# Issue order at the change of row tiles: both weight splits first, late rows centred on ScalarE and transposed one step earlier

## The chip, the cores and the metric

The kernel runs on one core of one Trainium2 chip. The metric is the device time of one execution in microseconds (us); shorter is better. The core's engines are called as the profile calls them: PE is TensorE (matmuls, with PEld for its weight loads), DVE is VectorE, ACT is ScalarE, POOL is GpSimd, and SP issues most of the DMAs. Each engine works through its own instructions in the order in which the program gives them; an instruction that waits holds up everything behind it on that engine.

## The reference

Two stages are computed. The first is an attention with 32 packed queries, done twice; the second is a block with a two-dimensional Fourier transform, a normalisation and a feed-forward pair of matrices. Cut to what matters:

```python
p_packed = softmax(p @ k.T / 8) @ v                # 8 batches, 8 heads, 576 rows, 64 wide
x = softmax(q @ p_packed.T / 8) @ p_packed         # then (8, 576, 512)
u = x + real(fft(fft(x, axis=1), axis=2))
un = (u - mean(u)) / sqrt(var(u) + 1e-6)           # along the 512 columns
out = u + maximum(un @ w_ch1, 0) @ w_ch2           # 512 -> 2048 -> 512
```

All inputs and outputs are float32.

## The kernel before

The 8 x 576 output rows are handled as 36 blocks of 128 rows, and four blocks make a **tile**: there are 9 tiles, 0 to 8, of 512 rows. `front(b)` computes the blocks of batch `b` up to `u`. `ffn` runs one tile through the feed-forward pair, and between its steps it advances `front` of the next batch, so that the rows of the next tile come into being while the present one is multiplied.

Every float32 product that must be exact is made of three matmuls on parts: a value is split into a high part (rounded) and a low part (the rest), and high x high, high x low and low x high are added up. `split` (lines 100 to 102) makes them: ACT copies the high part, and DVE or POOL subtracts it.

- **Weights.** The two matrices are held as 16 pieces each, `w1f` and `w2f` (128 x 512). Each tile splits them anew, because the split parts would not fit: the generator `wsplits` (line 633) yields one piece at a time, ACT makes `wr_h` and POOL makes `wr_l`. The order is w1(0), w1(1), w2(0), w1(2), w2(1) and so on to w2(15), then w1(0) of the next tile. The parts share six buffers (`wr`), three pairs, so a new pair takes the place of the pair three pieces earlier.
- **Steps of a tile.** For each of the 16 values of `j`, `up(j)` does 12 matmuls of 512 columns into the bank `ph`; ACT makes `hh` of it, DVE makes `hl`; and `down(j - 1)` does 12 matmuls into four banks `acc`. PE sees up(0), up(1), down(0), up(2), down(1), ..., up(15), down(14), down(15), and then up(0) of the next tile. After `up(j)` and after `down(j - 1)` the program asks `wsplits` for one piece each. After down(15) DVE adds `acc` to `u` (line 723), four instructions, and the rows are written out.
- **Rows of the next tile.** `Turned` brings the next tile's four blocks into the layout that `up` needs: centred (`un` = u minus its mean), transposed, and split into `uh` and `ul` (`parts(i)`, ACT and DVE). A pair of blocks that was ready earlier is centred by `less_quarters` on ACT, turned on DVE and by 16 small DMAs into `raw`. A pair whose second block is computed in the present tile's last steps is called **late**: `less(i)` centres it on DVE, and `moves(i)` transposes it on PE, four 128 x 128 transposes into `untp`. Late pairs exist for the tiles 1, 2 and 3; the tiles 4 to 8 get all four blocks from `raw`.
- **Statistics.** Some steps after a block is made, ACT sums its squares (`junk`, line 208), DVE scales them, and POOL raises the result to the power -1/2 (line 212, called the power below). The result is first used when the block's own tile ends, a tile later.

Tile 0's instructions are put in order by a scheduler. From tile 1 on, PE, DVE, ACT and POOL follow the order in which the code is written (`manual_schedule`), so that the place of a call in `ffn` decides what an engine does first. In this text w2(15) is the last weight piece of a tile, w1(0)' and w1(1)' are the first two of the next, and up(0)' is its first step.

Before the change the last step of a tile (`j == 15`) stands so: up(15), split of w2(15), then for late pairs `less(2)` and `less(3)`, `parts(0)` and `parts(1)`, a step of `front` (with the powers that are due), down(14) with the transposes of block 2 behind its 9th to 12th matmul, `parts(2)`, split of w1(0)', a step, down(15) with the transposes of block 3, `parts(3)`, split of w1(1)'.

Of the kernel before, what the change touches and what calls it, by code (L numbers as in the profile page):

```python
# [13 lines left out]
AF = mybir.ActivationFunctionType  # L14
ALU = mybir.AluOpType
# [35 lines left out]
NJ = 16  # L51
# [28 lines left out]
def tile_kernel(ctx, tc, kpT, qT, v, w1, w2, tabs, tabR, tabB, tabT, sel, ident_d, out):  # L80
    nc = tc.nc
# [95 lines left out]
    u_of, stat_of, place_of, free = {}, {}, {}, list(range(NU))  # L177
# [403 lines left out]
    class Turned:  # L581
# [8 lines left out]
            k = [key for key in self.keys[2 * h:2 * h + 2] if key[0] == b and key[1] != "R"]  # L590
            return "late" if any(key[2] == 1 for key in k) else "new" if k else "old"

        def less(self, i):
            key = self.keys[i]
            self.un[i] = work.tile([P, DM], F32, tag="ln", name="un")
            nc.vector.tensor_scalar(self.un[i], u_of[key], stat_of[key][:, 1:2], None, ALU.add)

        def moves(self, i):
            un, tp = self.un[i], bank("untp")
# [34 lines left out]
    def wsplits():  # L634

        for _ in tiles:
            for n, j in [(0, 0)] + [x for j in range(1, NJ) for x in ((0, j), (1, j - 1))] + [(1, NJ - 1)]:
                hi = work.tile([P, DM], F32R, tag="wr", name="wr_h", bufs=6)
                lo = work.tile([P, DM], F32R, tag="wr", name="wr_l", bufs=6)
                split(hi, lo, (w1f, w2f)[n][:, j, :], nc.gpsimd)  # L640
                ready.append((hi, lo))
                yield

    def ffn(first, turned, step, nxt, alone, following):
        keys = turned.keys
        n = len(keys)
        T = n * P
        uh, ul = turned.hl
        acc = [psf.tile([P, DM], F32, tag=f"acc{i}", name=f"acc{i}") for i in range(n)]
        now["acc"] = acc  # L650

        def up(j):
            wh, wl = ready.pop(0)

            pool, tag = (ps, "ps") if alone and j % 2 else (psf, "ph")
            ph = pool.tile([P, 512], F32, tag=tag, name="ph")

            step = T // 2 if first == 0 and j < SPL else T
            order = sorted(range(12), key=lambda k: k % 3 == 1) if j == 0 else range(12)
            for t in (slice(i, i + step) for i in range(0, T, step)):  # L660
                for n, k in enumerate(order):
                    c, (l, r) = k // 3, ((wh, uh), (wh, ul), (wl, uh))[k % 3]
                    nc.tensor.matmul(ph[:, t], l[:, c * P:(c + 1) * P], r[:, c, t], start=(n == 0), stop=(n == 11))  # L663
            hh = work.tile([P, 512], F32R, tag="hh", name="hh")
            hl = work.tile([P, 512], F32R, tag="hl", name="hl")
            nc.scalar.activation(hh[:, :T], ph[:, :T], AF.Relu)  # L666
            nc.vector.scalar_tensor_tensor(hl[:, :T], ph[:, :T], 0.0, hh[:, :T].bitcast(F32), ALU.max, ALU.subtract)  # L667
            return hh, hl

        def down(j, hh, hl, moves=()):  # L670

            moves = list(moves)
            vh, vl = ready.pop(0)
            for i in range(n):
                w = slice(i * P, (i + 1) * P)
                for k, (l, r) in enumerate(((hh, vh), (hh, vl), (hl, vh))):
                    nc.tensor.matmul(acc[i], l[:, w], r, start=(j == 0 and k == 0), stop=(j == NJ - 1 and k == 2))  # L677
                    if moves:
                        moves.pop(0)()

        kinds = [nxt.kind(h, following) for h in range(2)] if nxt else []
        assert kinds in ([], ["new", "late"], ["old", "new"], ["old", "old"]), kinds

        prev = None
        late = "late" in kinds
        for j in range(NJ):
            last = nxt is not None and j == NJ - 1
            cur = up(j)
            next(splits, None)
            if last:  # L690
                if late:
                    nxt.less(2)
                    nxt.less(3)
                nxt.parts(0)
                nxt.parts(1)
            step(2 * j)
            if j == 11:
                for h in range(2):
                    if kinds[h:h + 1] == ["old"]:
                        nxt.less_quarters(h)  # L700
                        nxt.turn(h)
            if prev is not None:
                down(j - 1, *prev, [lambda: None] * 8 + nxt.moves(2) if last and late else ())
                if j == 13:
                    for h in range(2):
                        if kinds[h:h + 1] == ["new"]:
                            nxt.less_quarters(h)
                if last:
                    nxt.parts(2)
                next(splits, None)  # L710
            step(2 * j + 1)
            if j == 13:
                for h in range(2):
                    if kinds[h:h + 1] == ["new"]:
                        nxt.turn(h)
            prev = cur
        down(NJ - 1, *prev, nxt.moves(3) if late else ())
        if nxt:
            nxt.parts(3)
        next(splits, None)  # L720
        for i, key in enumerate(keys):
            u = u_of[key]
            nc.vector.scalar_tensor_tensor(u, acc[i], stat_of[key][:, 2:3], u, ALU.mult, ALU.add)
            nc.sync.dma_start(out[(first + i) * P:(first + i + 1) * P, :], u)
            free.append(place_of[key])
# [24 lines left out]
    ready, splits = [], wsplits()  # L750
    next(splits)
    next(splits)
    for t, (first, tk) in enumerate(tiles):

        gen = front(t + 1) if t + 1 < B else iter(())
        ended = []

        def step(i):

            next_step()  # L760
            if t > 0 and i in (0, 2):
                next(rest, None)
            elif not ended and next(gen, None) == "rest":
                ended.append(gen)
            if t == 0 and i % 2 == 0 and i // 2 + LEAD < NJ:
                load_weights(i // 2 + LEAD)
            assert i < 2 * NJ - 1 or t + 1 >= B or ended

        nxt = Turned(tiles[t + 1][1]) if t + 1 < len(tiles) else None

        with tc.manual_schedule(engines=MANUAL) if t > 0 else nullcontext():
            ffn(first, cur, step, nxt, t + 1 >= B, t + 1)
        cur, rest = nxt, gen
# [112 lines left out]
```

## Time and profile before

| | |
|---|---|
| time, median of 3 runs | 1018.25 us (1017.5 to 1019.1) |
| the profiled execution's own time | 1017.34 us |
| its span, first to last instruction | 1015.6 us |
| granted PE clock, mean over the span | 0.983 |
| DVE busy | 582.9 us (57%) |
| ACT busy | 459.2 us (45%) |
| POOL busy | 474.6 us (47%) |

A page of the profile describes one execution. In a timeline each row is one instruction, or several alike: its start in us from the start of the span, its duration, engine, line, operation, what it writes and reads, and in brackets how long the engine had been idle before it and what it had waited for. The duration of a matmul covers its way through the array, and the next one starts before it has ended; the distance from start to start says how fast PE goes. In the list of waits a row gives who waited for whom, the total, how often, and the longest. In the windows a row gives the length of a stretch, each engine's busy time in it with the number of instructions, and then the granted PE clock, the DMA engines' busy share, and GB/s.

### The profile page before, as it was taken

The page shows a single profiled execution, that of the slowest core. Times are in us where ns is not written, and L with a number is a line of the kernel's source. Part 1 is how long each engine was busy: PE and PEld are TensorE (multiplying, and loading weights), DVE is VectorE, ACT ScalarE, POOL GpSimd, SP SyncE. Part 2 cuts the span into 40 slices and gives each one's busy share as a digit, 9 for nine tenths or more (in the row PEclk, how much of TensorE's full clock was granted, in tenths as well). Part 3 has the DMA queues.
Part 4 walks back from the last instruction along what each step waited for, and adds up shares of the span by engine and source line. Part 5 has one row for each costly group of instructions (what it writes and reads, how often), then busy time and mean ns, then how long its engine had stood idle before and what let it go on. Part 6 is the DMA issues. An engine that isn't in the chain of part 4 may idle for free.

```text
span 1015.6 us, 15016 instructions
## 1 busy us (share of the span) xinstructions
PE 957.9 (94%) x5588; PEld 782.3 (77%) x5588; DVE 582.9 (57%) x1227; ACT 459.2 (45%) x936; POOL 474.6 (47%) x426
## 2 busy tenths in 40 slices
PE   4199889999999999999999999999999999999998
PEld 2177668878877888788877887788778878888886
DVE  4885864559455856578456946595558562123112
ACT  4578634444453435445444445444534453333322
POOL 3715734364345534454355434643455344445443
PEclk9599989999999999999999999999999999999999
DMA  9367401220042001300140013101410010001001
GB/s 360 114 186 277 129 1 46 94 72 1 1 130 81 1 1 58 128 1 12 56 165 1 1 57 129 47 1 46 136 50 1 22 63 1 1 27 57 0 1 42
DMA packets 28169, 65.93 MB, mean 65 GB/s; under 512 B 5494, under 2 KB 12992, under 8 KB 28096
## 3 DMA queue, kind: packets, MB, share of 16 engines
q1 hardware_dynamic: 27120, 63.53, 18.8%
q0 software_dynamic: 976, 1.44, 0.5%
q8 instruction: 44, 0.72, 0.3%
q14 instruction: 29, 0.24, 0.1%
HBM read 48.70 MB, written 9.44 MB: 57 GB/s over the span
## 4 chain that ended last, share of the span: by engine, by line
PE 71%; DVE 8%; issue 7%; POOL 5%; ACT 3%; SPq 3%; DMA 2%; DVEq 0%; POOLq 0%; ACTq 0%
PE ph L663 32%; PE acc L677 28%; POOL wr_l L102 3%; SPq L623 3%; DVE turned L410 1%; PE po L317 1%; PE s L260 1%; DVE turned L406 1%; ACT hh L666 1%; PE py L228 1%; PE py L230 1%; PE py L229 1%; PE e1tp L294 1%; DMA ubuf<-w 1%; PE pz L228 1%
## 5 line engine op out<-in xcount | busy, mean ns | idle before, releaser
L102 POOL TENSOR_TENSOR wr_l<-w1f,wr_h 128x512 fp32r<-128x512 f32 x144 | 191.0, 1329 | 355.3 <-ACT wr_h L101 350.9
L667 DVE SCALAR_TENSOR_TENSOR hl<-ph,hh 128x512 fp32r<-128x512 f32 x144 | 98.9, 687 | 324.2 <-ACT hh L666 323.9
L102 POOL TENSOR_TENSOR wr_l<-w2f,wr_h 128x512 fp32r<-128x512 f32 x144 | 191.9, 1333 | 104.0 <-ACT wr_h L101 93.9
L663 PE MATMUL ph<-uh,wr_h 128*128 128x512 f32 (+1 forms) x580 | 229.5, 396 | 11.3 <-DVE hl L667 8.9
L663 PE MATMUL ph<-uh,wr_l 128*128 128x512 f32 (+1 forms) x580 | 226.6, 391 | 4.6 <-POOL wr_l L102 4.6
L677 PE MATMUL acc<-wr_h,hh 128*128 128x512 f32 x576 | 226.4, 393 | 0.4 <-ACT hh L666 0.4
L677 PE MATMUL acc<-wr_l,hh 128*128 128x512 f32 x576 | 225.7, 392 | 0.2 <-POOL wr_l L102 0.2
L677 PE MATMUL acc<-wr_h,hl 128*128 128x512 f32 x576 | 225.2, 391 | 0.0
L663 PE MATMUL ph<-ul,wr_h 128*128 128x512 f32 (+1 forms) x580 | 221.2, 390 | 0.0
L666 ACT ACTIVATE hh<-ph 128x512 fp32r<-128x512 f32 x144 | 86.0, 597 | 289.0 <-PE ph L663 288.7
L663 PEld LDWEIGHTS ph<-uh,wr_h 128*128 128x128 f32 x580 | 109.5, 189 | 46.2 <-DVE hl L667 10.3
L663 PEld LDWEIGHTS ph<-uh,wr_l 128*128 128x128 f32 x580 | 109.3, 188 | 29.7 <-POOL wr_l L102 6.6
L677 PEld LDWEIGHTS acc<-wr_h,hh 128*128 128x128 f32 x576 | 108.3, 188 | 23.5 <-ACT wst L171 0.8
L663 PEld LDWEIGHTS ph<-ul,wr_h 128*128 128x128 f32 x580 | 109.1, 189 | 22.0 <-DVE mx L279 0.8
L677 PEld LDWEIGHTS acc<-wr_h,hl 128*128 128x128 f32 x576 | 108.1, 188 | 22.7
L677 PEld LDWEIGHTS acc<-wr_l,hh 128*128 128x128 f32 x576 | 108.2, 188 | 22.1 <-POOL wr_l L102 0.6
L101 ACT CAST wr_h<-w1f 128x512 fp32r<-128x512 f32 x144 | 88.3, 613 | 10.7 <-PE acc L677 7.2
L101 ACT CAST wr_h<-w2f 128x512 fp32r<-128x512 f32 x144 | 89.1, 619 | 8.3 <-PE ph L663 6.7
L228 PE MATMUL py<-gh,fh 128*128 128x258 f32 x64 | 18.7, 294 | 27.5 <-ACT fh L470 27.5
L208 ACT ACTIVATE junk<-ubuf,stat 128x512 f32<-128x512 f32 x36 | 25.8, 719 | 36.2 <-DVE stat L204 36.2
L212 POOL TENSOR_TENSOR stat<-stat,mhalf 128x1 f32<-128x1 f32 x36 | 25.1, 707 | 30.8 <-DVE stat L211 30.6
L102 POOL TENSOR_TENSOR gl<-turned,gh 128x516 fp32r<-128x516 f32 x16 | 25.8, 1614 | 22.4 <-ACT gh L101 21.8
(201 smaller groups left out, 1286.6 us busy)
## 6 DMA issues: line engine op xcount, KB each, us to landing
kp<-kpT SPq DMA_DIRECT2D x16, 608.0 KB, 3.9
out<-ubuf SPq DMA_DIRECT2D x36, 256.0 KB, 2.1
vt<-v SPq DMA_DIRECT2D x14, 640.0 KB, 4.5
wst<-w SPq DMA_DIRECT2D x17, 512.0 KB, 4.7
qt<-qT SPq DMA_DIRECT2D x14, 576.0 KB, 4.4
raw<-flip SPq DMA_DIRECT2D x208, 32.0 KB, 1.8
ubuf<-w SPq DMA_DIRECT2D x9, 512.0 KB, 3.6
w1f<-w SPq DMA_DIRECT2D x3, 512.0 KB, 13.6
```

The lines of the kernel that those rows point to most:

```text
L101: nc.scalar.copy(hi, src)
L102: (lo_eng or nc.vector).tensor_tensor(lo, src, hi.bitcast(F32), ALU.subtract)
L208: nc.scalar.activation(junk, u, AF.Square, bias=st[:, 1:2], scale=1.0, accum_out=st[:, 2:3])
L212: nc.gpsimd.tensor_tensor(st[:, 2:3], st[:, 2:3], mhalf, ALU.pow)
L228: nc.tensor.matmul(o, lh, rh, start=first, stop=False)
L229: nc.tensor.matmul(o, lh, rl, start=False, stop=False)
L230: nc.tensor.matmul(o, ll, rh, start=False, stop=last)
L623: nc.sync.dma_start(raw[32 * q:32 * (q + 1), a].rearrange("p n x -> p (n x)"), flip[32 * a:32 * (a + 1), q].rearrange("p n x -> p (n x)"))
L663: nc.tensor.matmul(ph[:, t], l[:, c * P:(c + 1) * P], r[:, c, t], start=(n == 0), stop=(n == 11))
L666: nc.scalar.activation(hh[:, :T], ph[:, :T], AF.Relu)
L667: nc.vector.scalar_tensor_tensor(hl[:, :T], ph[:, :T], 0.0, hh[:, :T].bitcast(F32), ALU.max, ALU.subtract)
L677: nc.tensor.matmul(acc[i], l[:, w], r, start=(j == 0 and k == 0), stop=(j == NJ - 1 and k == 2))
```

## The change

In the last step of a tile, the split of w1(0)' is issued directly behind the split of w2(15), ahead of `parts(0)` and `parts(1)` and of the step that issues the powers. `parts(3)` moves up behind `parts(2)`, ahead of down(15). Late blocks are centred by ACT instead of DVE, at the end of the last step but one. The transposes of both late blocks stand within down(14), behind its matmuls 1 to 4 and 9 to 12; down(15) has none.

```diff
-        def less(self, i):
+        def less(self, i, scalar=False):
             key = self.keys[i]
             self.un[i] = work.tile([P, DM], F32, tag="ln", name="un")
-            nc.vector.tensor_scalar(self.un[i], u_of[key], stat_of[key][:, 1:2], None, ALU.add)
+            if scalar:
+                nc.scalar.activation(self.un[i], u_of[key], AF.Identity, bias=stat_of[key][:, 1:2], scale=1.0)
+            else:
+                nc.vector.tensor_scalar(self.un[i], u_of[key], stat_of[key][:, 1:2], None, ALU.add)
...
             if last:
-                if late:
-                    nxt.less(2)
-                    nxt.less(3)
+                next(splits, None)
                 nxt.parts(0)
                 nxt.parts(1)
             step(2 * j)
...
             if prev is not None:
-                down(j - 1, *prev, [lambda: None] * 8 + nxt.moves(2) if last and late else ())
+                down(j - 1, *prev, nxt.moves(2) + [lambda: None] * 4 + nxt.moves(3) if last and late else ())
...
                 if last:
                     nxt.parts(2)
-                next(splits, None)
+                    nxt.parts(3)
+                else:
+                    next(splits, None)
+                if late and j == NJ - 2:
+                    nxt.less(2, True)
+                    nxt.less(3, True)
             step(2 * j + 1)
...
-        down(NJ - 1, *prev, nxt.moves(3) if late else ())
-        if nxt:
-            nxt.parts(3)
+        down(NJ - 1, *prev)
         next(splits, None)
```

The lines behind the edit have numbers 3 or 4 higher in the changed kernel (up's matmul is L663 before and L666 after, down's L677 and L680, `hh` L666 and L669).

On ACT, where tile 3 ends (all blocks from `raw`), the order before is this, from `hh` of up(15) to `hh` of up(0)':

```order
L666 ACTIVATE hh<-ph 128x512
L101 CAST wr_h<-w2f 128x512
L101 CAST uh<-raw 128x4x4x32 x3
L101 CAST wr_h<-w1f 128x512
L101 CAST uh<-raw 128x4x4x32
L101 CAST wr_h<-w1f 128x512
L666 ACTIVATE hh<-ph 128x512
```

In the changed kernel the same place reads:

```order
L669 ACTIVATE hh<-ph 128x512
L101 CAST wr_h<-w2f 128x512
L101 CAST wr_h<-w1f 128x512
L101 CAST uh<-raw 128x4x4x32 x4
L101 CAST wr_h<-w1f 128x512
L669 ACTIVATE hh<-ph 128x512
```

The first cast of `w1f`, that of w1(0)', has moved from behind three `uh` casts to ahead of all four.

On POOL, where tile 1 ends, the order before is this; the second w2 row is w2(15), and the two w1 rows behind the powers are w1(0)' and w1(1)':

```order
L212 TENSOR_TENSOR stat<-stat,mhalf 128x1 x2
L102 TENSOR_TENSOR wr_l<-w2f,wr_h 128x512 x2
L212 TENSOR_TENSOR stat<-stat,mhalf 128x1 x2
L102 TENSOR_TENSOR wr_l<-w1f,wr_h 128x512 x2
L102 TENSOR_TENSOR wr_l<-w2f,wr_h 128x512
```

In the changed kernel:

```order
L212 TENSOR_TENSOR stat<-stat,mhalf 128x1 x2
L102 TENSOR_TENSOR wr_l<-w2f,wr_h 128x512 x2
L102 TENSOR_TENSOR wr_l<-w1f,wr_h 128x512
L212 TENSOR_TENSOR stat<-stat,mhalf 128x1 x2
L102 TENSOR_TENSOR wr_l<-w1f,wr_h 128x512
L102 TENSOR_TENSOR wr_l<-w2f,wr_h 128x512
```

The split of w1(0)' now stands ahead of the two powers, directly behind that of w2(15); that of w1(1)' stays behind them. The order is the same where the tiles 2 to 6 end.

On ACT, where tile 1 ends (blocks 0 and 1 from `raw`, blocks 2 and 3 late), before, from the last splits of step 14 on:

```order
L101 CAST wr_h<-w2f 128x512
L208 ACTIVATE junk,stat<-ubuf,stat 128x512 x2
L666 ACTIVATE hh<-ph 128x512
L101 CAST wr_h<-w2f 128x512
L101 CAST uh<-raw 128x4x4x32 x2
L101 CAST uh<-untp 128x4x4x32
L101 CAST wr_h<-w1f 128x512
L101 CAST uh<-untp 128x4x4x32
L101 CAST wr_h<-w1f 128x512
```

And in the changed kernel:

```order
L101 CAST wr_h<-w2f 128x512
L597 ACTIVATE un<-ubuf,stat 128x512 x2
L208 ACTIVATE junk,stat<-ubuf,stat 128x512 x2
L669 ACTIVATE hh<-ph 128x512
L101 CAST wr_h<-w2f 128x512
L101 CAST wr_h<-w1f 128x512
L101 CAST uh<-raw 128x4x4x32 x2
L101 CAST uh<-untp 128x4x4x32 x2
L101 CAST wr_h<-w1f 128x512
```

Two centrings have come in ahead of the sums of squares and of `hh`, and the cast of w1(0)' has moved ahead of the `uh` casts. The order of SP's DMAs is the same in both kernels.

## The prediction

> **What bounds the kernel now.** I read the page's first part, then who waits for whom on PE, then the timeline of PE around each change of tiles, and last the other engines there.
>
> ```profile
> PE 957.9 (94%) x5588; PEld 782.3 (77%) x5588; DVE 582.9 (57%) x1227; ACT 459.2 (45%) x936; POOL 474.6 (47%) x426
> ...
> PE py L228 <- ACT fh L470: 27.5, 2, 26.0
> PE ph L663 <- DVE hl L667: 8.9, 4, 5.1
> PE ph L663 <- POOL wr_l L102: 4.6, 5, 1.5
> PE untp L603 <- DVE un L596: 1.6, 2, 0.8
> ```
>
> PE is busy 94% of the span, so only its waits and its work can be shortened. The two largest waits end, by the timeline, before tile 1 begins: they belong to the start and to tile 0, and the change leaves them alone. The last two rows are the places that it edits: five waits of up's matmul for a POOL split, and two of a transpose for DVE's centring. Here are the five, each as the first two matmuls of up(0)' (the third of the first case too):
>
> ```profile
> 509.20 0.39 PE L663 MATMUL ph<-uh,wr_h 128*128 128x512 f32 x1
> 511.12 0.50 PE L663 MATMUL ph<-uh,wr_l 128*128 128x512 f32 x1 [1.53 <-POOL wr_l L102]
> 511.46 0.39 PE L663 MATMUL ph<-uh,wr_h 128*128 128x512 f32 x1
> ...
> 617.52 0.49 PE L663 MATMUL ph<-uh,wr_h 128*128 128x512 f32 x1
> 618.36 0.50 PE L663 MATMUL ph<-uh,wr_l 128*128 128x512 f32 x1 [0.35 <-POOL wr_l L102]
> ...
> 724.49 0.39 PE L663 MATMUL ph<-uh,wr_h 128*128 128x512 f32 x1
> 725.90 0.50 PE L663 MATMUL ph<-uh,wr_l 128*128 128x512 f32 x1 [1.02 <-POOL wr_l L102]
> ...
> 832.13 0.39 PE L663 MATMUL ph<-uh,wr_h 128*128 128x512 f32 x1
> 834.01 0.50 PE L663 MATMUL ph<-uh,wr_l 128*128 128x512 f32 x1 [1.49 <-POOL wr_l L102]
> ...
> 923.90 0.39 PE L663 MATMUL ph<-uh,wr_h 128*128 128x512 f32 x1
> 924.47 0.50 PE L663 MATMUL ph<-uh,wr_l 128*128 128x512 f32 x1 [0.18 <-POOL wr_l L102]
> ```
>
> These are the ends of tiles 3 to 7. The idle time in brackets is too small for what a stall costs, since PE would have started the next matmul before the last one ended. What one matmul takes undisturbed stands in a window of tile 8, where PE never pauses:
>
> ```profile
> 128.00:140.00 12.00, 6.93 (x30) 5.85 (x30) 11.26 (x38) 4.63 (x9) 6.46 (x7) 0.72 0.00 1
> ...
> 928.00:1004.00 76.00, 76.00 (x337) 62.91 (x336) 10.32 (x15) 23.16 (x43) 36.66 (x29) 1.00 0.02 7
> ```
>
> 76.00 us / 337 = 0.23 us from start to start. So the stalls are the distances less 0.23: 1.92, 0.84, 1.41, 1.88 and 0.57 give 1.69 + 0.61 + 1.18 + 1.65 + 0.34 = 5.47 us. The third matmul follows the second by 0.34 us, not 0.23: a restart costs 0.11 more, five times 0.55 us. Together **6.0 us**.
>
> The ends of tiles 0, 1 and 2, which have late rows, as the first matmul of down(14) and of up(0)':
>
> ```profile
> 180.01 0.39 PE L677 MATMUL acc<-wr_h,hh 128*128 128x512 f32 x1
> 186.40 0.39 PE L663 MATMUL ph<-uh,wr_h 128*128 128x512 f32 x1
> ...
> 287.13 0.39 PE L677 MATMUL acc<-wr_h,hh 128*128 128x512 f32 x1
> 294.58 0.40 PE L663 MATMUL ph<-uh,wr_h 128*128 128x512 f32 x1
> ...
> 395.47 0.39 PE L677 MATMUL acc<-wr_h,hh 128*128 128x512 f32 x1
> 402.90 0.40 PE L663 MATMUL ph<-uh,wr_h 128*128 128x512 f32 x1
> ```
>
> The same 24 matmuls and 8 transposes take 6.39, 7.45 and 7.43 us. The scheduler issued tile 0's centring early, and nothing waits there; so a change of tiles with late rows and no stall is seen in this very trace. The tiles 1 and 2 lose 1.06 + 1.04 = **2.1 us**.
>
> **The change part by part.** *The split of w1(0)' goes ahead.* The other engines where tile 3 ends:
>
> ```profile
> 503.93 0.60 ACT L666 ACTIVATE hh<-ph 128x512 fp32r<-128x512 f32 x1 [1.17 <-PE ph L663]
> 504.43 0.62 ACT L101 CAST wr_h<-w2f 128x512 fp32r<-128x512 f32 x1
> 505.12 1.30 POOL L102 TENSOR_TENSOR wr_l<-w2f,wr_h 128x512 fp32r<-128x512 f32 x1 [2.88 <-ACT wr_h L101]
> 507.03 0.62 ACT L101 CAST uh<-raw 128x512 fp32r<-128x512 f32 x1 [0.95 <-DMA raw<-flip]
> 507.56 0.62 ACT L101 CAST wr_h<-w1f 128x512 fp32r<-128x512 f32 x1
> 507.71 2.11 POOL L212 TENSOR_TENSOR stat<-stat,mhalf 128x1 f32<-128x1 f32 x2 [1.29 <-DVE stat L211]
> 508.08 0.61 ACT L101 CAST uh<-raw 128x512 fp32r<-128x512 f32 x1
> 509.80 2.53 POOL L102 TENSOR_TENSOR wr_l<-w1f,wr_h 128x512 fp32r<-128x512 f32 x2
> ```
>
> POOL is done with w2(15) at 506.42 and idles; then the two powers hold it for 2.1 us, and w1(0)' ends at about 511.1, where PE's wait ends. In the new order ACT casts w1(0)' right behind w2(15), from about 504.94 to 505.55. Its buffer pair was w1(15)'s, last read by up(15), which `hh` ahead of it waits for too: no new wait. POOL then splits it from 506.42 to 507.72. PE wants it one matmul after 509.20, at 509.43; 1.7 us to spare, so the whole stall goes. The powers come later, and their results are used a tile later: 0. w1(1)' stays behind them, for up(1)': 0.
>
> *What is late next.* `uh`: the third cast waits for SP's copies until 507.03. The fourth follows at once instead of behind w1(0)', so that all are done at about 508.2 rather than 508.7; the cast that went ahead fits into the 0.95 us that ACT idled. At PE's 509.20 that leaves 1.0 us. `ul` is wanted by the last four of up(0)'s matmuls, eight later: 509.20 + 8 x 0.23 = 511.0. Then come the banks: DVE's four additions free `acc`, which the next scores use.
>
> *Centring on ACT, transposes in down(14).* At the end of tile 1:
>
> ```profile
> 284.64 0.72 ACT L208 ACTIVATE junk<-ubuf,stat 128x512 f32<-128x512 f32 x1 [2.59 <-DVE stat L204]
> ...
> 287.33 0.60 ACT L666 ACTIVATE hh<-ph 128x512 fp32r<-128x512 f32 x1 [1.17 <-PE ph L663]
> ...
> 289.43 1.14 ACT L101 CAST uh<-raw 128x512 fp32r<-128x512 f32 x2 [0.98 <-DMA raw<-flip]
> ```
>
> The trace has no such centring on ACT in plain layout; between `hh` (0.60) and `junk` (0.72) stand its nearest rows, and I take 0.72, so two are 1.4 us. They wait for the same mean as `junk`: 284.64 to 286.1, the sums of squares to about 287.5, against PE's 287.33: `hh` of up(15) may be late by 0.2 us. Behind it queue w2(15), w1(0)', the `uh` casts and DVE's `hl`, but PE asks for `hh` only in down(15), after down(14)'s twelve matmuls and eight transposes (about 3.7 us). Cost 0; without that cover, 1.4 us twice. The first transpose stands behind PE's 287.13 + 0.23, when `un` has been ready for a microsecond or more. The number of transposes is the same. DVE loses its two centrings, which frees it for `ul`: nothing on PE. In tile 0, without a stall, nothing is to be won.
>
> *Sum.* 6.0 + 2.1 = 8.1 us less. Against the profiled execution, 1017.34 - 8.1 = 1009.2; that execution lies 0.9 us below the median of the runs, 1018.25 - 8.1 = 1010.1. I forecast a median, **1010.0 us**, and for this case alone 1009.0 to 1011.5: the runs of before differ by about 0.8 us to each side.
>
> **The rivals.** *Port turns (part of the gain).* Two POOL splits now stand back to back just where DVE subtracts four `ul`.
>
> ```profile
> 508.73 0.69 DVE L102 TENSOR_TENSOR ul<-raw,uh 128x512 fp32r<-128x512 f32 x1 [0.35 <-ACT uh L101]
> 509.34 2.72 DVE L723 SCALAR_TENSOR_TENSOR ubuf<-acc,stat,ubuf 128x512 f32<-128x512 f32 x4
> 515.54 0.34 PE L260 MATMUL acc<-kp 64*32 64x64 f32 x16
> ...
> 617.02 2.99 POOL L102 TENSOR_TENSOR wr_l<-w1f,wr_h 128x512 fp32r<-128x512 f32 x2
> 617.50 1.36 DVE L102 TENSOR_TENSOR ul<-raw,uh 128x512 fp32r<-128x512 f32 x1 [0.35 <-ACT uh L101]
> ```
>
> The last two rows are from the end of tile 4. A `ul` takes 0.69 us alone and 1.36 beside two splits, and those take 2.99 instead of 2.53: they hold each other up, in turns. If all four `ul` were slowed so, the last would end at 509.42 + 4 x 0.67 = 512.1, and PE would wait 1.1 us at each of the five ends without late rows; the scores (515.54, then 513.7) shift along with it. 5 x 1.1 = 5.5 us lost: 1015.6; with two or three ends hit, 1012.3 to 1013.4. Against it: one `ul` already bears such a delay, and the fourth now starts 0.5 us earlier. Chance 0.14.
>
> The Trainium skill speaks against this change here: "SBUF — State Buffer", section "SBUF: two separate sides", says that VectorE (with two SBUF inputs) and GpSimd share a port pair that is locked for a whole instruction, the other one blocked meanwhile. The trace's 1.36 against 0.69 agrees. By that rule alone, with a fair turn, the time is this rival's; with GpSimd first each time, the next one's.
>
> *POOL first each time (slower).* The same place, but DVE waits out a full POOL instruction, 1.30 us, for each `ul`: 509.42 + 4 x 1.30 = 514.6, less the 0.67 that one bears already, 513.9, so PE waits 2.9 us at each of five ends, 14.5 in all: 1024.6. It turns into a loss from 8.1 / 5 = 1.6 us at each end. Against it, 2.99 for the pair: POOL too gave way in between. Chance 0.05.
>
> *The stall only changes its name (no change).* The `uh` casts end as late as the split did, because SP's copies land later or ACT is held; the order of instructions is new, the time of PE isn't. At the ends of tiles 3 to 7 nothing is won; at those of 1 and 2 the copies' wait (289.43) is 4 us ahead of PE, so 2.1 us stay: 1016.1, at the edge of what can be told from before. Against it stands the 1.0 us to spare worked out above. Chance 0.09.
>
> *Clock.* With its pauses gone PE might be granted less. The rows above say the opposite: 0.72 in the window with long pauses, 1.00 in the one that is full. With the unnamed rest, 0.04, half slower, half same.
>
> **How the numbers follow.** Forecast 0.68, port turns 0.14, no change 0.09, POOL first 0.05, rest 0.04. The range reaches from 1008.2 (1009.2 less about 1 us, the spread of the runs) to 1014.5, which takes in most of the port turns; about 0.8 of the chance lies inside. A measurement of this kernel can tell about 0.2%, 2.0 us, from no change. Faster by more: 0.68 + 0.14 = 0.82. Within: 0.09 + 0.02 = 0.11. Slower: 0.05 + 0.02 = 0.07.
>
> **What would show it.** Right: the rows "PE ph <- POOL wr_l" and "PE untp <- DVE un" are gone or down to tenths, down(14) to up(0)' takes 6.4 us at the ends of tiles 1 and 2, the first two matmuls of up(0)' start 0.23 us apart, and PE's busy time stays at 958 us. Port turns: PE waits for `ul` or the scores wait for `acc`, and `ul` rows of 1.3 us stand beside POOL. No change: "PE ph <- ACT uh" comes in at the place of POOL. The forecast is wrong if PE's waits elsewhere grow by what these lose, such as for `hl` in the first steps of a tile, where the other engines have so far had the stall to catch up. Tile 1, entered without a stall, shows no such wait.

## The result and the profile after

| | before | changed |
|---|---|---|
| time, median (range, runs) | 1018.67 us (1017.35 to 1019.72, 6) | 1009.94 us (1009.34 to 1012.11, 6) |
| ratio, 95% interval | | 0.9919 (0.9906 to 0.9931) |
| the profiled execution's own time | 1017.34 us | 1010.0 us |
| its span | 1015.6 us | 1008.2 us |
| mean granted PE clock | 0.983 | 0.980 |

The change is faster by 0.81%, with the interval 7.0 to 9.6 us of 1018.67; 1010.0 was forecast. First the engines' busy time and then the waits that matter, from the page and the list of waits of the changed kernel:

```profile
PE 958.7 (95%) x5588; PEld 785.6 (78%) x5588; DVE 581.5 (58%) x1221; ACT 462.4 (46%) x942; POOL 479.0 (48%) x426
...
PE py L228 <- ACT fh L470: 27.1, 2, 25.6
...
PE ph L666 <- DVE hl L670: 7.1, 3, 4.5
...
PE ph L666 <- DVE s L365: 2.0, 6, 0.3
...
PE ph L666 <- ACT uh L101: 0.6, 1, 0.6
```

PE works as long as before (958.7 us). The row of `ph` waiting for POOL's `wr_l` (4.6 us, five times) and that of `untp` waiting for DVE's `un` (1.6 us, twice) are gone. The row of `uh`, which would have been the sign of "the stall only changes its name", is a single 0.6 us at the start of tile 0, where before has one as well (0.5 us).

The end of tile 3, PE first, then ACT, POOL and DVE, from the timeline of the changed kernel:

```profile
508.11 0.39 PE L666 MATMUL ph<-uh,wr_h 128*128 128x512 f32 x1
508.34 0.39 PE L666 MATMUL ph<-uh,wr_l 128*128 128x512 f32 x1
...
503.88 0.62 ACT L101 CAST wr_h<-w1f 128x512 fp32r<-128x512 f32 x1
505.99 1.14 ACT L101 CAST uh<-raw 128x512 fp32r<-128x512 f32 x2 [0.45 <-DMA raw<-flip]
...
504.06 1.31 POOL L102 TENSOR_TENSOR wr_l<-w2f,wr_h 128x512 fp32r<-128x512 f32 x1 [2.88 <-ACT wr_h L101]
505.33 1.76 POOL L102 TENSOR_TENSOR wr_l<-w1f,wr_h 128x512 fp32r<-128x512 f32 x1
507.78 1.59 POOL L212 TENSOR_TENSOR stat<-stat,mhalf 128x1 f32<-128x1 f32 x2 [0.69 <-DVE stat L211]
...
505.05 2.59 DVE L102 TENSOR_TENSOR ul<-raw,uh 128x512 fp32r<-128x512 f32 x2 [0.85 <-DMA raw<-flip]
507.69 1.27 DVE L102 TENSOR_TENSOR ul<-raw,uh 128x512 fp32r<-128x512 f32 x2
508.89 2.71 DVE L727 SCALAR_TENSOR_TENSOR ubuf<-acc,stat,ubuf 128x512 f32<-128x512 f32 x4
```

The first two matmuls of up(0)' start 0.23 us apart, where it was 1.92. The split of w1(0)' ends at 507.09, a microsecond ahead of PE; the powers stand behind it.

The end of tile 1 (late rows), PE from the first matmul of down(14) to that of up(0)', and then ACT:

```profile
288.08 0.39 PE L680 MATMUL acc<-wr_h,hh 128*128 128x512 f32 x1
288.31 0.27 PE L606 MATMUL untp<-ident,un 128*128 128x128 f32 x1
...
294.51 0.39 PE L666 MATMUL ph<-uh,wr_h 128*128 128x512 f32 x1
...
282.90 0.72 ACT L597 ACTIVATE un<-ubuf,stat 128x512 f32<-128x512 f32 x1
285.58 0.72 ACT L597 ACTIVATE un<-ubuf,stat 128x512 f32<-128x512 f32 x1 [1.96 <-DVE stat L204]
286.21 0.71 ACT L208 ACTIVATE junk<-ubuf,stat 128x512 f32<-128x512 f32 x1
288.28 0.60 ACT L669 ACTIVATE hh<-ph 128x512 fp32r<-128x512 f32 x1 [0.56 <-PE ph L666]
```

6.43 us instead of 7.45. The second centring ends at 286.30, two microseconds before the first transpose.

**Where the time went.** The first up(0) begins anywhere between 63.6 and 66.2 us in the executions profiled here, and the change leaves that part alone. So two executions are compared from up(0) of tile 1 to the end of the span: 1015.6 - 186.40 = 829.2 us before, 1008.2 - 187.29 = 820.9 after, a difference of **8.3 us** (the spans differ by 7.4, since this execution reached tile 1 0.9 us later). By the starts of up(0) in the two timelines, tile by tile:

| tile | before, us | after, us | less | predicted |
|---|---|---|---|---|
| 1 (late rows) | 108.18 | 107.22 | 0.96 | 1.06 |
| 2 (late rows) | 108.32 | 107.30 | 1.02 | 1.04 |
| 3 | 106.30 | 106.30 | 0.00 | 0 |
| 4 | 108.32 | 106.31 | 2.01 | 1.69 + 0.11 |
| 5 | 106.97 | 106.21 | 0.76 | 0.61 + 0.11 |
| 6 | 107.64 | 106.29 | 1.35 | 1.18 + 0.11 |
| 7 | 91.77 | 89.92 | 1.85 | 1.65 + 0.11 |
| 8, to the end | 91.7 | 91.4 | 0.3 | 0.34 + 0.11 |

(A stall at the end of tile 3 falls into the time of tile 4, since up(0)' has begun. The spans are given to a tenth, and so is the last row.) The terms come out one by one: 6.3 us from the splits where 6.0 was predicted, 2.0 from the late rows where it was 2.1. The last row falls short by about 0.15 us; the entry on port turns below says why.

### The profile page after: what moved, and what is told of

Same layout as the page of the kernel before. It is cut to its first block, busy times and chain, and to the rows that moved or that the text cites. A ratio compares the mean times of both kernels' runs of the same rounds, so it can differ in the third digit from the quotient of the medians.

```text
span 1008.2 us, 15014 instructions
## 1 busy us (share of the span) xinstructions
PE 958.7 (95%) x5588; PEld 785.6 (78%) x5588; DVE 581.5 (58%) x1221; ACT 462.4 (46%) x942; POOL 479.0 (48%) x426
## 4 chain that ended last, share of the span: by engine, by line
PE 82%; DVE 6%; issue 5%; POOL 3%; ACT 2%; DMA 2%; POOLq 0%; DVEq 0%; ACTq 0%
PE ph L666 36%; PE acc L680 33%; POOL wr_l L102 2%; DVE turned L410 1%; PE po L317 1%; DVE turned L406 1%; PE s L260 1%; PE px L229 1%; PE px L228 1%; PE px L230 1%; PE py L228 1%; PE e1tp L294 1%; PE py L229 1%; PE py L230 1%; PE pz L228 1%
## 5 line engine op out<-in xcount | busy, mean ns | idle before, releaser
L102 POOL TENSOR_TENSOR wr_l<-w1f,wr_h 128x512 fp32r<-128x512 f32 x144 | 193.9, 1347 | 353.3 <-ACT wr_h L101 348.8
L666 PE MATMUL ph<-uh,wr_h 128*128 128x512 f32 (+1 forms) x580 | 229.7, 396 | 9.7 <-DVE hl L670 7.1
L680 PE MATMUL acc<-wr_h,hh 128*128 128x512 f32 x576 | 226.7, 394 | 0.4 <-ACT hh L669 0.4
L666 PE MATMUL ph<-uh,wr_l 128*128 128x512 f32 (+1 forms) x580 | 226.7, 391 | 0.0
L680 PE MATMUL acc<-wr_l,hh 128*128 128x512 f32 x576 | 225.7, 392 | 0.2 <-POOL wr_l L102 0.2
L680 PE MATMUL acc<-wr_h,hl 128*128 128x512 f32 x576 | 225.2, 391 | 0.0
L666 PE MATMUL ph<-ul,wr_h 128*128 128x512 f32 (+1 forms) x580 | 221.8, 391 | 0.0
L669 ACT ACTIVATE hh<-ph 128x512 fp32r<-128x512 f32 x144 | 86.0, 597 | 285.3 <-PE ph L666 285.1
L666 PEld LDWEIGHTS ph<-uh,wr_h 128*128 128x128 f32 x580 | 109.7, 189 | 44.0 <-DVE hl L670 8.2
L666 PEld LDWEIGHTS ph<-uh,wr_l 128*128 128x128 f32 x580 | 109.6, 189 | 23.5
L666 PEld LDWEIGHTS ph<-ul,wr_h 128*128 128x128 f32 x580 | 109.3, 189 | 22.3 <-DVE mx L279 0.8
L680 PEld LDWEIGHTS acc<-wr_h,hh 128*128 128x128 f32 x576 | 108.3, 188 | 23.6 <-ACT wst L171 0.8
L680 PEld LDWEIGHTS acc<-wr_h,hl 128*128 128x128 f32 x576 | 108.1, 188 | 22.9
L680 PEld LDWEIGHTS acc<-wr_l,hh 128*128 128x128 f32 x576 | 108.4, 188 | 22.1 <-POOL wr_l L102 0.6
```

The source lines that it names most:

```text
L102: (lo_eng or nc.vector).tensor_tensor(lo, src, hi.bitcast(F32), ALU.subtract)
```

## The experiments

Each kernel was timed against the kernel before on its own chip, whose median there was 1018.34 to 1019.18 us. "From tile 1 on" is the difference to the 829.2 us, from the profiles. Six questions were open: which half gives what, what held the split, whether engine or place matters in the late half, whether the transposes' place matters, why the halves do not add up, and whether the waits that are left can be removed.

| kernel | median, us | ratio (95%) | from tile 1 on |
|---|---|---|---|
| e1, splits only | 1012.02 | 0.9933 (0.9919 to 0.9946) | -5.9 |
| e2, late rows only | 1018.04 | 0.9994 (0.9984 to 1.0004) | -0.2 |
| e3, before with powers later | 1014.06 | 0.9951 (0.9939 to 0.9964) | -4.7 |
| e4, before with cast early | 1016.89 | 0.9987 (0.9978 to 0.9995) | -1.3 |
| e5, centring on DVE | 1009.78 | 0.9908 (0.9895 to 0.9922) | -8.2 |
| e6, transposes at old places | 1010.0 | 0.9911 (0.9898 to 0.9925) | -7.8 |
| e7, products on POOL | 1009.06 | 0.9907 (0.9894 to 0.9921) | -10.2 |
| e8, e7 and rests on POOL | 1010.91 | 0.9920 (0.9906 to 0.9935) | -9.0 |
| e9, the changed kernel again | 1009.75 | 0.9912 (0.9899 to 0.9925) | -8.2 |
| e10, e7 again | 1008.75 | 0.9899 (0.9882 to 0.9916) | -9.9 |
| e11, late rows and powers later | 1012.55 | 0.9942 (0.9928 to 0.9955) | -5.8 |

### The two halves: e1 and e2

e1 is the kernel before with the split of w1(0)' ahead; the centring, its engine and the transposes stay.

```diff
             if last:
+                next(splits, None)
                 if late:
                     nxt.less(2)
                     nxt.less(3)
...
                 if last:
                     nxt.parts(2)
-                next(splits, None)
+                else:
+                    next(splits, None)
```

> The kernel before with the weight splits alone moved: w1(0)' directly behind w2(15). Centring on VectorE in the last step, transposes and the last parts stay where they were. Theory (seven separate stalls, five of them for the split): the five waits of up's matmul for a POOL split go, 6.0 us less than before, ratio 0.994; the two waits of a transpose for the centring stay at 0.8 us each in the list of waits (7.4 us from down(14) to up(0)'). Rival (port turns): VectorE's low parts beside the two POOL splits end late and PE waits for them, up to 5.5 us given back, ratio 0.9995. Rival (one cause: ScalarE is overfull at a tile's end and it is the centring's move that helps): no gain, ratio 1.000.

Measured: 5.9 us from tile 1 on, and the second matmul of up(0)' follows at 0.23 us at every end. In its list of waits the row of `ph` for POOL's `wr_l` is gone, and the late rows' wait stays to the tenth:

```profile
PE untp L603 <- DVE un L596: 1.6, 2, 0.8
```

So the splits' half is 5.9 of the 8.3 us by itself. The five ends without late rows give 6.2 of it (506.4 us from up(0) of tile 4 to the end before, 500.2 here). The tiles 1 and 2 come out 0.26 us longer together: down(14) to up(0)' takes 7.58 and 7.57 us there, against 7.45 and 7.43. There DVE's two centrings now stand beside two POOL splits instead of one. DVE at the end of tile 1, before and then in e1:

```profile
288.57 1.93 DVE L596 TENSOR_SCALAR un<-ubuf,stat 128x512 f32<-128x512 f32 x2
...
289.98 2.98 DVE L596 TENSOR_SCALAR un<-ubuf,stat 128x512 f32<-128x512 f32 x2
```

So the two halves meet here as well: on top of e1 the late half is worth 8.3 - 5.9 = 2.4 us.

e2 is the changed kernel with the split of w1(0)' back at its old place.

```diff
             if last:
-                next(splits, None)
                 nxt.parts(0)
                 nxt.parts(1)
...
                     nxt.parts(2)
+                next(splits, None)
+                if last:
                     nxt.parts(3)
-                else:
-                    next(splits, None)
```

> The kernel before with the late rows alone moved: centred on ScalarE in the last step but one, transposed in down(14), fourth parts ahead of down(15); w1(0)' is split where it was, behind the third parts. Theory: the two waits of a transpose go, 2.1 us less than before, ratio 0.998, down(14) to up(0)' 6.4 us at the ends of tiles 1 and 2, and the five waits for the POOL split stay, 4.6 us in the list. Rival (the waits hide one another): with the transposes no longer late, up(0)' of tiles 2 and 3 comes a microsecond earlier and waits there for the split of w1(0)', which ends at about 294.2 in the trace of before against 293.8 then wanted: 0.4 us each comes back, ratio 0.9985.

The theory missed: 1018.04 against 1018.34 us, no difference that can be told, where about 2 us were to come. The rival on record, that one wait hides the other, had 0.4 us coming back at each of two ends. Tile 1 is shorter by 1.0 us (107.20) and tile 2 by 0.6 (107.76), but the wait for POOL has grown. The list of waits of e2, its PE and its POOL where tile 1 ends:

```profile
PE ph L666 <- POOL wr_l L102: 6.0, 6, 1.6
...
293.87 0.39 PE L666 MATMUL ph<-uh,wr_h 128*128 128x512 f32 x1
294.46 0.50 PE L666 MATMUL ph<-uh,wr_l 128*128 128x512 f32 x1 [0.20 <-POOL wr_l L102]
...
292.08 1.07 POOL L212 TENSOR_TENSOR stat<-stat,mhalf 128x1 f32<-128x1 f32 x2 [1.95 <-DVE stat L211]
293.11 2.56 POOL L102 TENSOR_TENSOR wr_l<-w1f,wr_h 128x512 fp32r<-128x512 f32 x2
```

Two things happen. In the tiles with late rows PE now reaches up(0)' before the split is ready, where the transposes' wait had covered it: the second matmul comes 0.36 and 0.26 us late at the ends of the tiles 1 and 2, as that rival said. Neither foresaw that the stalls at the other ends came out larger: by the starts they were 1.71, 1.37, 1.33, 1.73 and 0.48 us here, 6.6 in all, where the one execution of before had 5.47. So the 0.2 us of e2 and the 5.9 of e1 do not add up to 8.3. e11 asks below what the late rows are worth when POOL is out of their way.

### What held the split: e3 and e4

Before the change POOL idled 1.29 us, then did two powers, and then split w1(0)'; ACT's cast for it stood behind three `uh`. Each of these is taken away alone. In e3, of before, the powers are due one step later (whose results are used a tile later).

```diff
         after(1, squares)
-        after(2, deviation)
+        after(3, deviation)
```

> The kernel before, with nothing moved but the powers (and their scaling on VectorE), one step of front later everywhere: at the end of a tile they come behind the split of w1(0)' on POOL, while ScalarE still casts w1(0)' behind three casts of uh. This asks what held the split: POOL's two powers or ScalarE's late cast. Theory (the powers at the ends of tiles 3, 5 and 6, the cast at those of 4 and 7, by the rows of before): stalls of 1.7, 1.2 and 1.65 us fall to 0.0 to 0.2, those of 0.6 (tile 4) and 0.3 (tile 7) stay; 4.5 us less, ratio 0.9956. Rival (the cast is what counts everywhere): ratio 1.000. Rival (the powers everywhere): 6.0 us less, ratio 0.994.

The stalls go from 1.69, 0.61, 1.18, 1.65, 0.34 to 0.20, 0.58, 0, 0, 0.17 us. ACT and POOL at the end of e3's tile 3:

```profile
508.71 0.62 ACT L101 CAST uh<-raw 128x512 fp32r<-128x512 f32 x1 [0.98 <-DMA raw<-flip]
509.24 0.62 ACT L101 CAST wr_h<-w1f 128x512 fp32r<-128x512 f32 x1
...
509.93 1.30 POOL L102 TENSOR_TENSOR wr_l<-w1f,wr_h 128x512 fp32r<-128x512 f32 x1 [1.86 <-ACT wr_h L101]
511.19 1.51 POOL L212 TENSOR_TENSOR stat<-stat,mhalf 128x1 f32<-128x1 f32 x2
```

POOL is now free ahead of the split and waits for ACT's cast, which stands behind a `uh` that waits for a copy of SP's. What is left is the second cause, and it varies with when the copies land.

In e4, of before, the split moves only from behind down(14) to ahead of it: still behind the powers, but its cast earlier.

```diff
             step(2 * j)
+            if last:
+                next(splits, None)
...
                 if last:
                     nxt.parts(2)
-                next(splits, None)
+                else:
+                    next(splits, None)
```

> The kernel before, with the split of w1(0)' ahead of down(14) and of the third parts, but behind the step that issues the powers: ScalarE casts w1(0)' behind two casts of uh instead of three, POOL still splits it behind the powers. The counterpart of the run with the powers later. Theory: the stalls at the ends of tiles 3, 5 and 6 stay as they were, that of tile 7 (no powers there) goes, that of tile 4 shrinks by 0.1 us at most: 0.5 us less, ratio 0.9995, not to be told from 1. Rival (the cast is what counts): 6.0 us less, ratio 0.994.

It gains 1.3 us where 0.5 was expected, and the powers keep the rest. ACT, DVE, POOL and PE at the end of e4's tile 3:

```profile
508.54 0.62 ACT L101 CAST wr_h<-w1f 128x512 fp32r<-128x512 f32 x1
...
510.06 0.20 DVE L211 TENSOR_SCALAR stat<-stat 128x1 f32<-128x1 f32 x2
510.28 1.68 POOL L212 TENSOR_TENSOR stat<-stat,mhalf 128x1 f32<-128x1 f32 x2 [1.29 <-DVE stat L211]
511.94 2.54 POOL L102 TENSOR_TENSOR wr_l<-w1f,wr_h 128x512 fp32r<-128x512 f32 x2
...
513.27 0.50 PE L663 MATMUL ph<-uh,wr_l 128*128 128x512 f32 x1 [1.12 <-POOL wr_l L102]
```

The cast is done at 509.16, the split starts at 511.94: POOL waits for DVE's scaling (L211, done at 510.26), then does the powers, and PE waits 1.12 us. The five stalls are 1.28, 0.92, 1.16, 1.03 and 0 us by the starts; that of tile 4 is larger than the 0.61 of before. So there were two causes: the powers, without which the ends of the tiles 5 and 6 have no stall at all, and the cast behind `uh`, which keeps 0.20, 0.58 and 0.17 us at those of 3, 4 and 7. The change's place for the split is ahead of both, and no copy of SP's stands before it.

### Engine or place: e5 and e6

In e5, of the changed kernel, DVE centres the late rows, at the new place.

```diff
-                    nxt.less(2, True)
-                    nxt.less(3, True)
+                    nxt.less(2)
+                    nxt.less(3)
```

> The changed kernel, with the late blocks centred on VectorE instead of ScalarE, at the same place in the program (end of the last step but one). Theory (the place of the centring is what removes the wait of the transposes, the engine is free): VectorE has the mean itself and 3 us without other work there, so that the centred rows are ready before down(14); the same time as the changed kernel, 1010.0 +- 0.7 us, ratio to before 0.992. Rival (VectorE cannot take it there: beside POOL's split of w2(14) each centring lasts up to 1.4 us, and hl of up(15) comes late): a wait of a transpose of some tenths at the ends of tiles 1 and 2, at most 1 us lost.

1009.78 us, and 8.2 less from tile 1 on: the engine makes no difference that shows. e5's DVE at the end of tile 1:

```profile
284.69 1.73 DVE L599 TENSOR_SCALAR un<-ubuf,stat 128x512 f32<-128x512 f32 x2
```

Both blocks are centred by 286.42, and PE's first transpose starts at 287.47. So 1.0 us is to spare, where ACT in the changed kernel left 2.0 (286.30 and 288.31): less, but enough.

In e6, of the changed kernel, the transposes and `parts(3)` are back at their old places; the early centring on ACT stays.

```diff
-                down(j - 1, *prev, nxt.moves(2) + [lambda: None] * 4 + nxt.moves(3) if last and late else ())
+                down(j - 1, *prev, [lambda: None] * 8 + nxt.moves(2) if last and late else ())
...
-                    nxt.parts(3)
...
-        down(NJ - 1, *prev)
+        down(NJ - 1, *prev, nxt.moves(3) if late else ())
+        if nxt:
+            nxt.parts(3)
```

> The changed kernel, with the transposes where they were: block 2 behind the 9th to 12th matmul of down(14), block 3 in down(15), the fourth parts behind down(15). The centring stays early on ScalarE. Theory (the transposes waited for the centring alone; their place costs nothing): the same time as the changed kernel, ratio to before 0.992; 6.4 us from down(14) to up(0)' at the ends of tiles 1 and 2. Rival (the last block's uh is cast too late when it is transposed in down(15)): a wait for uh at up(0)' of tiles 2 and 3; by the rows of before uh was cast 1.5 us ahead of up(0)' with the 1.0 us stall, so 0 to 0.5 us each.

1010.0 us, 7.8 less from tile 1 on; the 0.5 us to the changed kernel lies within what two executions differ by. Its tiles 1 and 2, the ones with late rows, take 107.20 and 107.29 us, as in the changed kernel. Of the late half, then, the earlier place of the centring is what counts; the engine and the transposes' place add nothing that shows.

### Why the halves do not add: e11

e11 is e2 with e3's edit: the late half, and the split of w1(0)' at its old place with no powers ahead of it.

```diff
-        after(2, deviation)
+        after(3, deviation)
```

> The late rows alone moved, and the powers one step of front later: the two runs in one. The late rows alone gave 0.6 us in the profile where 2.1 were expected; up(0)' of tiles 2 and 3 then waited 0.36 and 0.26 us for the split of w1(0)', and later ends waited longer than in the profile of before. Theory (the parts share a cause: the late rows' gain is held back by the split behind the powers): with the powers out of the way the waits at the ends of tiles 1 and 2 are gone, tiles 1 and 2 take 107.2 and 107.3 us from up(0) to up(0)', and the gains add up, 4.9 + 2.1 = 7.0 us, ratio 0.993. Rival (the late rows are worth little by themselves): 5.0 us as with the powers alone, ratio 0.995.

The tiles 1 and 2 take 107.17 and 107.26 us, as in the changed kernel: with POOL free the late rows give all of their 2 us. The total is 5.8 us from tile 1 on, where 7.0 was expected, and the interval of the ratio holds both the theory's 0.993 and the rival's 0.995; the times of the tiles decide between them. What is missing lies at the ends 3 to 7, which keep stalls of 0.2 to 0.6 us (0.19, 0.34, 0.33, 0.42, 0.61), with POOL waiting for the late cast by its rows at those of 3 to 6. The list of waits of e11 shows four of them:

```profile
PE ph L666 <- POOL wr_l L102: 1.0, 4, 0.4
```

So the covering in the tiles 1 and 2 is settled. The other stalls grew in both pairs: e2's five add up to 6.6 us against 5.5 before, and e11's to 1.9 against 0.95 in e3. The traces show part of the way. At the end of tile 5 ACT's third cast of `uh`, which waits for a copy of SP's, starts 2.02 us ahead of up(0)' in e2 and e11, but 2.76 and 2.64 ahead in before and e3. In e11 that delays the cast of w1(0)'; in e2 it moves DVE's `ul` onto POOL's two splits, which take 3.06 us instead of 2.53. Why the copies land later stays open: the order there differs only in the place of `parts(3)`, and no run separates that from what two executions differ by.

### The waits that are left: e7, e8, e9 and e10

Six waits of 0.34 us stand in the changed kernel where up's matmul waits for DVE's transposes of the scores (`s`, L365), once in each of the tiles 1 to 6. The first of them, PE and then DVE:

```profile
214.21 1.06 PE L260 MATMUL s2T<-qt,ppT 64*32 64x512 f32 x16
215.62 0.47 PE L666 MATMUL ph<-uh,wr_h 128*128 128x512 f32 x1 [0.34 <-DVE s L365]
...
213.49 1.83 DVE L410 TENSOR_TENSOR turned<-turned 128x258 f32<-128x258 f32 x2
215.23 0.37 DVE L365 STREAM_TRANSPOSE s<-s2Tt 128x64 f32<-128x64 f32 x2
```

A sum and a difference of products (L410, the products for short) hold DVE ahead of the transposes. e7 is the changed kernel with both on POOL from tile 1 on (a table names the engine: 1 is DVE, 0 POOL).

```diff
-TA = (1, 1, 1)
+TA = (1, 1, 0)
```

> The changed kernel, and the sums and differences of the turned spectra (line 410, two of 128x258 per group) on POOL instead of VectorE in the tiles from 1 on. In the changed kernel six waits of 0.3 us are left, up's matmul for VectorE's transpose of s (line 365), which begins late because these two last 1.8 us there beside POOL's splits. Theory: with them off VectorE the transpose begins when the scores are done and the bank is free in time: six stalls of about 0.34 + 0.16 (overlap of the matmuls) + 0.1 (restart) go, 3.6 us less than the changed kernel, ratio to before 0.988. Rival (POOL becomes the bound: two of 0.7 us more between its weight splits): PE waits for a weight split in those steps, no gain or some us more.

The waits go, and e7's tiles 1 to 6 are each 0.30 to 0.36 us shorter, 2.0 us in all. Its POOL and DVE at the same place:

```profile
213.38 1.44 POOL L410 TENSOR_TENSOR turned<-turned 128x258 f32<-128x258 f32 x2
214.37 0.38 DVE L365 STREAM_TRANSPOSE s<-s2Tt 128x64 f32<-128x64 f32 x2 [1.08 <-PE s2Tt L260]
```

More had been expected, since the overlap of matmuls was added to each wait as in the prediction. Here the matmul ahead of the wait is the last of sixteen small ones, and the wait as printed is about all of the gain.

e8 adds the second table, in which 1 is POOL: it puts the twelve small operations of L446 to L459 that tile 0 advances on POOL, to shorten the start.

```diff
-ES = (1, 0, 0)
+ES = (1, 1, 0)
...
-TA = (1, 1, 1)
+TA = (1, 1, 0)
```

> As the kernel with the products' sums on POOL, and the twelve small operations per group that line up the rest columns (lines 446 to 459) on POOL instead of VectorE in tile 0 as well. In the changed kernel PE waits 4.5 us for hl in tile 0 (up to 133.9 us), where VectorE is busy 12.7 of 13 us, 3 us of it with these operations ahead of hl. Theory: hl comes 2 to 3 us earlier, ratio to before 0.988. Rival (POOL needs longer for them and its weight splits come late, or the scheduler fills VectorE with the next group's work): no gain, ratio 0.990.

1010.91 us: no gain. Its tile 0 took 125.69 us, against 122.49 in the changed kernel and in its second profile, e9, on the same chip. The wait for `hl` did not shrink, and a new wait came in. The rows of e8, and then that of e9:

```profile
PE ph L666 <- DVE hl L670: 8.8, 3, 5.9
...
PE pg L400 <- DVE turned L406: 1.0, 1, 1.0
...
PE ph L666 <- DVE hl L670: 8.4, 3, 5.1
```

Against e9 the two waits are 1.4 us of the 3.2. The rest is busy time of PE in tile 0, 115.48 us against 113.64 for the same matmuls at a granted clock of 0.96 and 0.97; what made it longer is not shown.

On that chip ran e9, the changed kernel as it is, and e10, e7 as it is.

> The changed kernel as it is, beside the two that follow on the same chip, so that differences of 0.2% between them can be read. Theory: ratio to before 0.992 +- 0.001.

> The kernel with the products' sums on POOL (line 410), beside the changed kernel on the same chip. Its profile had none of the six waits for the transpose of s, and its tiles 1 to 6 took 0.30 to 0.36 us less each, 2.0 us together, not the 3.6 that I expected. Theory: 2.0 us less than the changed kernel, ratio to before 0.990. Rival (the medians' difference of 0.9 us is all, POOL gives some back elsewhere): ratio 0.991 to 0.992, not to be told from the changed kernel.

1009.75 and 1008.75 us, and the times from tile 1 to the end of the span are 821.0 and 819.3. Twice, then, the profiles show e7 some 1.7 to 1.9 us shorter, and the medians 0.9 (e7 against 1009.94) and 1.0 us (e10 against e9); the intervals (0.9899 to 0.9925 and 0.9882 to 0.9916) overlap. e7 is the best version found, and by its times alone it is not told apart from the changed kernel.

## Why the prediction was right

- **The bound.** PE's waits at the change of tiles were what could be shortened, and nothing came in their place: its busy time stayed, and the total went down by what the waits were worth. The two large waits ahead of tile 1 stayed, as predicted.
- **The five stalls, 6.0 us.** Measured 6.3 between the two profiles and 6.2 at the same five ends of e1. Counting from start to start and adding the 0.11 of a restart was needed: the five idle times as printed come to 4.6. But that the number fell so close is luck in part: with the split at the same old place, e2's five stalls came to 6.6 us without the restarts. That the median came within 0.1 us of the forecast is luck too, since runs of the changed kernel spread over 2.8 us.
- **Why the split was late.** The prediction laid it to the powers, after POOL's idle 1.29 us. e3 and e4 show a second cause, the cast behind `uh` and SP's copies. The forecast did not hang on it, as it also had the cast ahead of the `uh`.
- **The 1.7 us to spare.** The split started directly behind that of w2(15), as predicted, but took 1.76 us instead of 1.30 and ended 1.25 us ahead of PE's 508.34; so three quarters of the margin were left.
- **The late rows, 2.1 us.** Measured 2.0, with the same signature as tile 0's end (6.43 and 6.39 us). e5 and e6 narrow it: the time of the centring, not its engine.
- **`hh` of up(15) late by 0.2 us.** It wasn't: ACT idled 0.56 us ahead of it. Only one of the two centrings waited for the new mean; the other ran at 282.90. The durations, taken as 0.72 from `junk`, were 0.72.
- **Port turns (0.14).** Its mechanism is in the trace and did not decide. While POOL splits, two `ul` take 2.59 us, against 1.27 for the two behind them; the last ends at 508.96, and PE wants it at 508.11 + 8 x 0.23 = 509.95. The rival had all four slowed. Only two met POOL's splits, which were over at 507.09; the other two stood beside the powers and kept to their 1.27. The Trainium skill's rule ("SBUF — State Buffer", section "SBUF: two separate sides"), by which one engine is blocked for the other's whole instruction, agrees with the longer durations; its price here was small because two of the four began when both splits were over. At the end of tile 7 there are no powers, and w1(1)' is split sooner. There the rival does cost something. PE, DVE and POOL:

```profile
918.74 1.19 PE L666 MATMUL ph<-ul,wr_h 128*128 128x512 f32 x4
...
913.77 4.91 DVE L102 TENSOR_TENSOR ul<-raw,uh 128x512 fp32r<-128x512 f32 x4 [0.85 <-ACT uh L101]
...
916.76 1.38 POOL L102 TENSOR_TENSOR wr_l<-w1f,wr_h 128x512 fp32r<-128x512 f32 x1 [0.95 <-ACT wr_h L101]
```

The four `ul` last until 918.68, and PE wanted them at 916.84 + 8 x 0.23 = 918.66; its four matmuls start at 918.74 and take 1.19 us, where they take 1.07 at the end of tile 3. That is about 0.2 us, and it fits the last row of the table (0.3 where 0.45 was predicted).
- **POOL first (0.05).** Under it POOL would lose nothing, yet its split took 1.76 us instead of 1.30: it gave way too.
- **The stall only changes its name (0.09).** PE waits for `uh` at no end of a tile. But e2 shows this rival's idea at work in the half that was taken as safe: there, one wait had covered another.
- **Clock.** 0.980 after and 0.983 before, on the whole span. Over 11 us where tile 3 ends, PE (the first busy time) went from 9.46 us to all of the window, and the clock (ahead of the last two numbers) stayed at 1.00. Before, then changed, from the windows:

```profile
503.00:514.00 11.00, 9.46 (x43) 7.51 (x43) 6.81 (x11) 4.38 (x9) 5.91 (x5) 1.00 0.52 172
```

```profile
503.00:514.00 11.00, 11.00 (x83) 8.66 (x82) 8.25 (x14) 5.96 (x12) 7.19 (x6) 1.00 0.49 165
```

## What to carry to other kernels

On an engine that works in order, look at what stands ahead of the instruction that is waited for, not only at that instruction: two tiny powers whose results are needed a tile later held a weight split that PE needed at once. Two waits ahead of one point cover each other, so an edit that gains nothing alone (e2) can be worth 2 us beside another one, and the halves are to be measured together as well as apart. A stall costs more than the idle time that the trace prints where long matmuls overlap (here 6.3 for 4.6 us), and no more than that behind a group of short ones.

## What the runs showed of the hardware

- A power on a 128 x 1 column is dear on POOL for its size. Where a tile ends, two in a row took 1.07 us (e2), 1.51 (e3), 1.59 (changed) and 2.11 (before), that is 0.8 to 1.6 times as long as the subtraction of a whole 128 x 512 piece (1.30). The spread goes with what DVE does meanwhile: one that stood beside no instruction of DVE took 0.54 to 0.57 us in every trace here, and the pair of 2.11 us stood beside two `ul` and the start of the additions. The list of instructions by source has the shortest, median and longest of the 36 in the changed kernel, in ns, and the timeline has one that stood alone:

```profile
L212 POOL TENSOR_TENSOR stat<-stat,mhalf x36: 543/568/1523, 61.2 to 842.9; 128x1 f32<-128x1 f32 x36
...
205.78 0.56 POOL L212 TENSOR_TENSOR stat<-stat,mhalf 128x1 f32<-128x1 f32 x1
```
